# Two attention decode problems on one core: V loaded once per group, half of K and V from the Pool queue

## Chip, cores and metric

The kernel runs on one core of a Trainium2 chip. The metric is the device time in microseconds (us) of one execution, as the median of three runs; less is better.

## What is computed

The same computation is done on two independent sets of inputs, A and B, and the two results are put side by side.

```
B, Hq, Hkv, Sk, Dh, D = 2, 32, 16, 16384, 128, 576
W = 4096                                   # the last W positions of the caches
q = (x @ wq)                               # one query token per batch entry, 32 heads
k, v = k_cache[:, :, Sk-W:], v_cache[:, :, Sk-W:]   # each of 16 heads serves 2 query heads
scores = einsum("bhqd,bhkd->bhqk", q, k) * Dh**-0.5
o = einsum("bhqk,bhkd->bhqd", softmax(scores), v)
out = o.reshape(B, 1, Hq*Dh) @ wo          # bf16 throughout, x: [2, 1, 576], out: [2, 1, 576]
```

Nearly all bytes are K and V: 2 problems x 2 tensors x 2 batch entries x 16 heads x 4096 x 128 x 2 bytes, 134 MB of the 153 MB that are read.

## The kernel before

**Groups and slabs.** Four heads of one problem make a group; there are NG = 8 groups. A group has a K slab and a V slab for each of the two batch entries, so there are 16 K slabs and 16 V slabs of 4 MB. A slab fills 128 partitions with 32 KB each: partition (r, k) holds 128 consecutive positions of head k (line 370). Four slabs fit in the tile `ring` (NSLOT = 4). K and V take the four slots in turn.

**The stream.** All large loads are issued by SyncE (SP), in the order of the list `stream` (lines 322 to 332): the K slab of step t, then the V slab of step t-3 (LAG = 3), with the rows of `wo` ("M", 2.25 MB for two groups) in between, and at the end the `wo` rows of the last two groups ("W"). SP waits before each load for the last reader of the slot (line 373): the transpose of a K slab (`last_reader`, line 440) or the matmuls of a V slab (line 551). It issues strictly in this order, so one late reader holds up all loads behind it. Both `wq` (4.5 MB each) come first; they lie in the ring too, and the first K slabs wait for the query matmuls `f_q` that read them (`first_deps`, line 342).

**One K slab, step t** (loop at line 700). `make_X` (line 432): VectorE transposes each half of the slab in 32x32 blocks of fp32 pairs into `xt`. `make_S` (line 442): 16 TensorE matmuls for each half, with the queries in `zq` (which `make_Z` on GpSimd (POOL) writes), give the scores in PSUM, `STT`, one buffer for each of two groups.

**A group's softmax** starts when its second K slab is through. `make_max` (line 468): a maximum on VectorE, two small steps on POOL; `make_Tm_pe`, `make_nM`, `make_bias` (lines 475 to 495): two small TensorE transposes with a VectorE and a POOL step between them turn it into the bias of the exponential. Then ScalarE does four exponentials of 128x512 (line 500), which write `pR` and sums; `make_pT` (line 506) transposes `pR` on VectorE into `pT`, of which there are two; `make_sums` forms the divisors.

**A group's V.** `make_PV` (line 544) multiplies a V slab: 32 matmuls whose stationary part is 128x32, in four column groups of the array. `make_evac` (line 553) scales and sums the result on VectorE, `make_dg` and `make_pick` (lines 573, 582) sort it by head, and `make_projm` (line 622) multiplies by the `wo` rows. For the last two groups `make_proj` (line 645) does this at the very end, followed by the output in `make_E`.

**Order.** The program is written out by hand: each engine executes its own list in the order in which the helpers are called, and waits on semaphores. What stands behind a waiting instruction waits too, the loads on SP and the steps on POOL among them. The end of the program after the loop (lines 741 to 770) is also written out by hand. `filler` matmuls compute nothing that is used.

The DMA call for one slab:

```
return e.dma_start(ring[:, r, c0 * 128:c1 * 128],
                   src[:, :, c0:c1, :].rearrange("r k j d -> r k (j d)")).then_inc(sm, 16)
```

Of the kernel before, what the change touches and what calls it, by code (L numbers as in the profile page):

```python
# [5 lines left out]
FP32 = mybir.dt.float32  # L6
# [57 lines left out]
def build_kernel(nc, probs, out):  # L64
    NSLOT = 4
    LAG = 3
# [27 lines left out]
    with es:  # L94
# [5 lines left out]
        pR = sb("pR", [128, 2048], BF16)  # L100
        pT = sb("pT", [128, 2, 2048], BF16)
        tmp = sb("tmp", [128, 512], FP32)
        oR = sb("oR", [128, Bb, 128], FP32)
# [4 lines left out]
        ones_f = sb("ones_f", [128, 128], FP32)  # L108
        ones_b = sb("ones_b", [128, 128], BF16)
        sel = sb("sel", [128, 4, 128], BF16)  # L110
        bmask = sb("bmask", [128, 4], FP32)
        vmask = sb("vmask", [128, 4], FP32)
        offm = sb("offm", [128, 4], FP32)
# [4 lines left out]
        m8 = sb("m8", [128, 16, 8], FP32)  # L118
        selx = sb("selx", [128, 8, 16], FP32)
        selm = sb("selm", [128, 16, 8], FP32)  # L120
        bsel = sb("bsel", [128, 2], FP32)
        hmask = sb("hmask", [4, 2], FP32)
        mx = sb("mx", [128, 2], FP32)
        mv = sb("mv", [128, 2], FP32)
        m1 = sb("m1", [128, 1], FP32)
        nM = sb("nM", [1, 16], FP32)
        nMrep = sb("nMrep", [1, 8, 16], FP32)
        bias4 = sb("bias4", [128, 4], FP32)
        rsum4 = sb("rsum4", [128, 4], FP32)
        rsum8 = sb("rsum8", [128, 2, 4], FP32)  # L130
        ssum = sb("ssum", [128, 2], FP32)
        rsb = sb("rsb", [128, 2, 2], FP32)
        oP = sb("oP", [128, 2, 8, Bb], BF16)
        oM = sb("oM", [128, 16, Bb], BF16)
        out_sb = sb("out_sb", [Bb, NOUT], BF16)
        out_w = sb("out_w", [32 + Bb, NH], BF16)
# [12 lines left out]
        pTf = pT[:].rearrange("p v f -> p (v f)")  # L149
# [3 lines left out]
        assert XW + 512 <= 2 * 2048  # L153
# [5 lines left out]
        ring_sem = [sem("ring%d" % r) for r in range(NSLOT)]  # L159
        v_cuts = [0, 80, KJ]  # L160
        lastv_sem = [sem("lastv")]
# [61 lines left out]
        def turn_x(P):  # L223
# [5 lines left out]
            def f_xT(e, P=P):  # L229
                for k in range(4):  # L230
# [8 lines left out]
        d_dm = mask(dmask[:, 0:4], ident_f[:].rearrange("p (c j q) -> p j c q", j=4, q=8), AX.XY, "dmask")  # L239
# [4 lines left out]
        p_offm = pool(lambda e: e.tensor_scalar(offm[:], vmask[:], -1.0, OFF, ALU.add, ALU.mult), [d_vm], "offm")  # L244
        p_v2 = pool(lambda e: e.tensor_tensor(v2[:], vmask[:, 0:2], vmask[:, 2:4], ALU.add), [d_vm], "v2")
        p_m8 = pool(lambda e: e.tensor_copy(m8[:], jmask_f[:, 0:8].unsqueeze(1).broadcast_to([128, 16, 8])), [d_jf], "m8")
        p_sx = pool(lambda e: e.tensor_copy(selx[:], jmask_f[:, 0:8].unsqueeze(2).broadcast_to([128, 8, 16])), [d_jf], "selx")
        p_sm = pool(lambda e: e.tensor_copy(selm[:].rearrange("p (a h) c -> p a h c", a=2),
                                            jmask_f[:, 0:8].unsqueeze(1).unsqueeze(3).broadcast_to([128, 2, 8, 8])), [d_jf], "selm")
# [72 lines left out]
        stream = []  # L322
        for t in range(NSLAB + LAG):
            if t < NSLAB:
                stream.append(("K", t))
            if t >= LAG:
                i = t - LAG
                if i % 4 == 0 and i > 0:
                    stream.append(("M", i // 4 - 1))
                stream.append(("V", i))  # L330
        stream.append(("W", NG - 2))
        stream.append(("W", NG - 1))
        NM = NG // 2 - 1
        slot_of = {}
        uses = {}
        n_slot = 0
        for key in stream:
            if key[0] in "KV":
                slot_of[key] = (n_slot + 3) % NSLOT
                uses.setdefault(slot_of[key], []).append(key)  # L340
                n_slot += 1
        first_deps = {0: [q_done[0]], 1: [q_done[0], q_done[1]], 2: [q_done[1]], 3: []}
        stream_dma = {}
        last_reader = {}
# [4 lines left out]
        def issue(key):  # L349
# [18 lines left out]
            P, g, b = i // (2 * GP), (i // 2) % GP, i % 2  # L368
            src_t = probs[P][1] if kind == "K" else probs[P][2]
            src = src_t[b, 4 * g:4 * g + 4, Sk - W:Sk, :].rearrange("k (r j) d -> r k j d", j=KJ)  # L370
            r = slot_of[key]
            prior = uses[r][:uses[r].index(key)]
            deps = [last_reader[prior[-1]]] if prior else first_deps[r]
            cuts = [(0, KJ, ring_sem[r])]
            if key == ("V", NSLAB - 1):
                cuts = [(v_cuts[k], v_cuts[k + 1], ([ring_sem[r]] + lastv_sem)[k]) for k in range(2)]
            stream_dma[key] = []
            for c0, c1, sm in cuts:
                def f(e, c0=c0, c1=c1, sm=sm):
                    return e.dma_start(ring[:, r, c0 * 128:c1 * 128],  # L380
                                       src[:, :, c0:c1, :].rearrange("r k j d -> r k (j d)")).then_inc(sm, 16)
                stream_dma[key].append((c0, c1, dma_op("sp", sm, 1, f, deps, "%s%d_%d" % (kind, i, c0))))
# [6 lines left out]
        def filler(n):  # L389
            def f(e):  # L390
                o = STT[(NG - 1) % 2][:, 0:512]
                last = e.matmul(o, ones_b[:, :], xt[:, 0, 0:512], start=True, stop=True, skip_group_check=True)
                for _ in range(n - 1):
                    last = mm_held(e, o, ones_b[:, :], xt[:, 0, 0:512], True)
                return last
            pe(f, [exp_op[NG - 1], Xop[(NSLAB - 1, 1)]], "filler")
# [17 lines left out]
        def make_Z(t):  # L414
            P, g, b = t // (2 * GP), (t // 2) % GP, t % 2
            deps = [qs_ev, p_zq, d_bm]
            if t >= 2:
                deps.append(Sop[(t - 2, 1)])

            def f(e):  # L420
                for kp in range(2):
                    m = 2 * b + kp
                    b0 = zq[:, 0, m, 16 + 4 * m:16 + 4 * m + 1]
                    dst = bass.AP(b0.tensor, b0.offset, [list(b0.ap[0]), [4 * 144, 4], [32, 4], [1, 4]])
                    o = b * Hq + 8 * g + 4 * kp
                    src = qs[:, P, :].rearrange("d (p w) -> d p w", p=4)[:, :, o:o + 4].unsqueeze(2).broadcast_to([128, 4, 4, 4])
                    msk = bmask[:, 0:4].unsqueeze(1).unsqueeze(3).broadcast_to([128, 4, 4, 4])
                    last = e.tensor_tensor(dst, src, msk, ALU.mult)  # L428
                return last
            Zop[t] = pool(f, deps, "Z%d" % t)  # L430

        def make_X(t, jh):
            ensure(("K", t))
            r = slot_of[("K", t)]
            deps = [stream_dma[("K", t)][0][2], Sop[(t - 1, jh)] if t >= 1 else d_xT[1]]
# [6 lines left out]
        def make_S(t, jh):  # L442
# [3 lines left out]
            if b == 0 and G >= 2:  # L446
                deps.append(exp_op[G - 2])
# [32 lines left out]
        def make_nM(G):  # L480
            n, b = tm_job[G]
            op = ch[(G, "Tm")]
            nm = dve(lambda e: e.tensor_reduce(nM[0:1, 0:16], b[0:1, 0:128].rearrange("o (a w) -> o w a", a=8), AX.X, ALU.max, negate=True),
                     [op] + prev(G, "nMrep"), "nM%d" % G)
            tb_consumer[n] = nm
            ch[(G, "nMrep")] = pool(lambda e: e.tensor_scalar(nMrep[:], nM[0:1, 0:16].unsqueeze(1).broadcast_to([1, 8, 16]), SCALE, None, ALU.mult),
                                    [nm] + prev(G, "bias"), "nMrep%d" % G)

        def make_bias(G):
            n, bk, op = tb_job(lambda e, bank: e.transpose(bank[:, 0:1], nMrep[0:1].rearrange("o a w -> o (a w)"), ident_f[0:1, 0:1]),  # L490
                               "bias%d" % G, [ch[(G, "nMrep")], p_ident_f])
            ch[(G, "bias")] = op
            b4 = dve(lambda e: e.scalar_tensor_tensor(bias4[:], vmask[:], bk[:, 0:1], offm[:], ALU.mult, ALU.add),  # L493
                     [op, p_offm, d_vm] + ([exp_op[G - 1]] if G >= 1 else []), "bias4_%d" % G)
            tb_consumer[n] = b4
            st = STT[G % 2]

            def f(e):
                for kv in range(4):
                    last = e.activation(pR[:].rearrange("p (x k) -> p k x", k=4)[:, kv, :],  # L500
                                        st[:, :].rearrange("p (x t) -> p t x", t=2)[:, kv % 2, :], ACTF.Exp,
                                        bias=bias4[:, kv:kv + 1], scale=SCALE, accum_out=rsum4[:, kv:kv + 1])
                return last
            exp_op[G] = act(f, [b4] + prev(G, "rsum8") + ([pT_op[G - 1]] if G >= 1 else []), "exp%d" % G)

        def make_pT(G):
            v = G % 2
            deps = [exp_op[G]] + ([PVop[2 * (G - 2) + 1]] if G >= 2 else [qt_op])
            pT_op[G] = dve(lambda e: e.transpose(  # L509
                pT[:, v, :].rearrange("p (w j q) -> p j w q", w=4, q=8),  # L510
                pR[:].rearrange("p (j w q) -> p j w q", w=4, q=8)), deps, "pT%d" % G)

        def make_rsum(G):
            ch[(G, "rsum8")] = pool(lambda e: e.tensor_tensor(
# [38 lines left out]
        def make_evac(i):  # L553
# [6 lines left out]
            if i:  # L560
                deps.append(ch["tmp"])
# [301 lines left out]
```

## Time and profile before

| | |
|---|---|
| median of 3 runs | 363.31 us (363.24 to 363.34) |
| time of the profiled execution | 363.1 us |
| its span, first to last instruction | 361.8 us |
| mean granted TensorE clock | 0.887 of full speed |
| busy: PE, DVE, ACT, POOL | 229.0, 218.6, 45.4, 24.3 us |
| bytes read | 153.10 MB, 423 GB/s over the span |
| time that packets of SP's DMA queue took | 98.7% of 16 DMA engines' span |

The span is what the profile's clock runs over; the time of the execution is 1.3 us longer. Busy times are those in which an engine executes something; waits are not counted. A DMA is issued by an engine's queue and then carried out by 16 DMA engines in packets, one packet here being one contiguous row of a partition. "DMA share" is the mean share of time in which these 16 were busy. The profile's timeline lists each instruction with its start and duration, and in brackets how long the engine had been idle before it and for what. Durations below come from this one execution.

### The profile page before, as it was taken

The numbers are of one execution on the slowest core, as the hardware profiler recorded it, in microseconds if no ns is written. First come the engines' busy times: TensorE is split into PE (matmuls) and PEld (weight loads), VectorE is DVE, ScalarE is ACT, GpSimd is POOL, SyncE is SP. The second block draws the span as 40 slices with busy tenths as digits, with TensorE's granted clock in tenths as the row PEclk, the third lists the DMA queues.
The fourth block names the chain that finished last, engine by engine and source line by source line (L and its number), as shares of the span: only waits on it lengthen the run. The fifth ranks groups of instructions, "written<-read, shape, count | busy, mean of one in ns | idle before, by whom it ended". The sixth has DMA issues, their size and how long they took to land.

```text
span 361.8 us, 2701 instructions
## 1 busy us (share of the span) xinstructions
PE 229.0 (63%) x1357; PEld 56.1 (16%) x943; DVE 218.6 (60%) x150; ACT 45.4 (13%) x77; POOL 24.3 (7%) x84
## 2 busy tenths in 40 slices
PE   0397687767464866671696656662776675667575
PEld 0010111112110211120121211110112121112222
DVE  0811898495949392924919493952927776675522
ACT  1002100040031002200005000500005000500500
POOL 4200101100010001000010000000010000001000
PEclk9999698969999889888798998899589897869989
DMA  8999999999999999999999999999999999999996
GB/s 327 449 428 420 442 426 424 446 413 446 417 447 420 442 422 422 439 438 420 438 424 434 431 438 412 448 420 442 424 435 429 428 438 420 434 442 420 427 417 258
DMA packets 6088, 153.28 MB, mean 424 GB/s; under 512 B 684, under 2 KB 828, under 8 KB 1084
## 3 DMA queue, kind: packets, MB, share of 16 engines
q1 hardware_dynamic: 6056, 153.10, 98.7%
q8 instruction: 9, 0.15, 0.2%
q14 instruction: 3, 0.02, 0.0%
q10 hardware_dynamic: 20, 0.01, 0.0%
HBM read 153.10 MB, written 0.00 MB: 423 GB/s over the span
## 4 chain that ended last, share of the span: by engine, by line
DMA 49%; DVE 24%; PE 16%; issue 8%; ACT 1%; POOL 1%; SPq 0%
DMA ring<-in_B_k_cache_dram 25%; DVE xt L436 15%; DMA ring<-in_B_v_cache_dram 9%; DMA ring<-in_B_wq_dram 7%; DMA ring<-in_A_k_cache_dram 6%; PE st L266 6%; PE st L462 5%; DMA wob<-in_B_wo_dram 3%; DVE oR L569 2%; DVE mx L470 2%; DVE pT L509 2%; PE pj L266 2%; DVE tmp L562 2%; PE ot L539 1%; ACT pR L500 1%
## 5 line engine op out<-in xcount | busy, mean ns | idle before, releaser
L462 PE MATMUL st<-xt,zq 128*128 128x512 bf16 x256 | 119.3, 466 | 93.6 <-DVE xt L436 93.6
L436 DVE STREAM_TRANSPOSE xt<-ring 128x4096 f32<-128x4096 f32 x32 | 141.6, 4429 | 33.5 <-DMA ring<-in_A_k_cache_dram 18.2
L266 PE MATMUL st<-xt,zq 128*128 128x512 bf16 x256 | 118.0, 461 | 0.0
L500 ACT ACTIVATE pR<-st,bias 128x512 bf16<-128x512 f32 x32 | 40.0, 1419 | 219.0 <-DVE bias L493 219.0
L462 PEld LDWEIGHTS st<-xt,zq 128*128 128x128 bf16 x256 | 28.3, 110 | 211.5 <-DVE xt L436 110.0
L539 PE MATMUL ot<-ring,pT 128*32 128x512 bf16 x512 | 32.0, 393 | 8.3 <-DMA ring<-in_B_v_cache_dram 8.3
L493 DVE SCALAR_TENSOR_TENSOR bias<-vmask,tb,offm 128x4 f32<-128x4 f32 x8 | 1.8, 224 | 37.1 <-PE tb L490 37.1
L523 DVE TENSOR_REDUCE ssum<-tb 128x2 f32<-128x8 f32 x8 | 1.3, 162 | 33.4 <-PE tb L520 33.4
L428 POOL TENSOR_TENSOR zq<-qs,bmask 128x64 bf16<-128x64 bf16 x32 | 8.6, 292 | 161.2 <-PE st L266 140.3
L509 DVE STREAM_TRANSPOSE pT<-pR 128x2048 bf16<-128x2048 bf16 x8 | 18.4, 2303 | 0.7 <-ACT pR L500 0.7
L562 DVE SCALAR_TENSOR_TENSOR tmp<-ot,rsb,dmask 128x512 f32<-128x512 f32 x16 | 11.5, 719 | 9.4 <-PE ot L539 9.4
L281 PE MATMUL ot<-ring,pT 128*32 128x512 bf16 x18 | 7.6, 421 | 15.1 <-DMA ring<-in_A_wq_dram 14.5
L539 PEld LDWEIGHTS ot<-ring,pT 128*32 128x32 bf16 x512 | 12.4, 99 | 23.7 <-DMA ring<-in_B_v_cache_dram 10.5
L569 DVE TENSOR_REDUCE oR<-tmp 128x128 f32<-128x512 f32 x15 | 15.6, 1039 | 0.5
L266 PE MATMUL pj<-ring,pT 128*32 128x512 bf16 x36 | 12.1, 422 | 0.0
L266 PE MATMUL pj<-wob,oM 128*2 128x288 bf16 (+1 forms) x64 | 10.2, 256 | 0.0
L470 DVE TENSOR_REDUCE mx<-st 128x2 f32<-128x1024 f32 x8 | 9.7, 1208 | 0.1
L500 ACT ACTIVATION_READ_ACCUMULATOR pR<-st,bias 128x1 f32 x32 | 9.1, 283 | 0.0
L636 PE MATMUL pj<-wob,oM 128*2 128x288 bf16 x32 | 7.9, 286 | 0.0
L224 DVE TENSOR_TENSOR xt<-xt,hmask 4x1152 bf16<-4x1152 bf16 x2 | 2.8, 1398 | 8.4 <-DMA xt<-in_A_x_dram 8.4
L266 PE MATMUL st<-ring,pT 128*32 128x512 bf16 x18 | 7.4, 414 | 0.0
L472 POOL TENSOR_TENSOR mv<-mx,v 128x2 f32<-128x2 f32 x8 | 1.6, 195 | 80.0 <-DVE mx L470 80.0
(71 smaller groups left out, 79.5 us busy)
## 6 DMA issues: line engine op xcount, KB each, us to landing
ring<-in_A_k_cache_dram SPq DMA_DIRECT2D x8, 4096.0 KB, 24.9
ring<-in_A_v_cache_dram SPq DMA_DIRECT2D x8, 4096.0 KB, 30.0
ring<-in_B_k_cache_dram SPq DMA_DIRECT2D x8, 4096.0 KB, 28.5
ring<-in_B_v_cache_dram SPq DMA_DIRECT2D x7, 4096.0 KB, 31.8
ring<-in_A_wq_dram SPq DMA_DIRECT2D x1, 4608.0 KB, 13.6
ring<-in_B_wq_dram SPq DMA_DIRECT2D x1, 4608.0 KB, 24.1
wob<-in_A_wo_dram SPq DMA_DIRECT2D x2, 2304.0 KB, 29.8
ring<-in_B_v_cache_dram SPq DMA_DIRECT2D x1, 2560.0 KB, 26.9
```

Source lines behind the costliest of these rows:

```text
L266: return e.add_instruction(mybir.InstMatmult(name=nc.get_next_instruction_name(), engine=mybir.EngineType.PE, ins=[e.lower_ap(mv_), e.lowe ...
L281: last = e.matmul(QB[c], wt, mv_, start=first, stop=True, skip_group_check=True)
L428: last = e.tensor_tensor(dst, src, msk, ALU.mult)
L436: Xop[(t, jh)] = dve(lambda e: e.transpose(xt[:, jh, :].bitcast(FP32).rearrange("p (kp x kt) -> p x kp kt", kp=2, kt=2), ring[:, r, jh * H ...
L462: last = e.matmul(ob, wt, mv_, start=first, stop=True, skip_group_check=True)
L470: ch[(G, "max")] = dve(lambda e: e.tensor_reduce(mx[:], st[:, :].rearrange("p (x t) -> p t x", t=2), AX.X, ALU.max), [Sop[(2 * G + 1, 1)]] ...
L500: last = e.activation(pR[:].rearrange("p (x k) -> p k x", k=4)[:, kv, :], st[:, :].rearrange("p (x t) -> p t x", t=2)[:, kv % 2, :], ACTF.Exp,
L509: pT_op[G] = dve(lambda e: e.transpose(pT[:, v, :].rearrange("p (w j q) -> p j w q", w=4, q=8), pR[:].rearrange("p (j w q) -> p j w q", w= ...
L539: last = e.matmul(OTB[32 * c:32 * c + 32, :], pT[:, v, base + 32 * c:base + 32 * c + 32], ring[:, r, jj * 128:(jj + 4) * 128], start=rd == ...
L562: evac_op[i] = dve(lambda e: e.scalar_tensor_tensor(tv, o, rsb[:, v, b:b + 1], dm, ALU.mult, ALU.mult), deps, "ev%d" % i)
L569: ch[(G, "red%d" % b)] = dve(lambda e: e.tensor_reduce(oR[:, b, :], tmp[:].rearrange("p (j d) -> p d j", j=4), AX.X, ALU.add), [evac_op[i] ...
L636: last = e.matmul(PJ[0], oM[:, j, :], mv_, start=start and j == 0, stop=True, skip_group_check=True)
```

## The change

- **V per group.** A V load now covers both batch entries of a group: 64 partitions for each, 64 KB in each partition (256 positions), 8 MB in two slots of the ring. There is one place for V (slots 2 and 3), for the last group slots 0 and 1. K slabs are cut by halves of these 256 positions rather than by batch entry, and take two slots (0 and 1; the first slab slot 3).
- **Two queues.** Of each K and V load SP issues partitions 32 to 95 (batch entry 0). POOL issues partitions 0 to 31 and 96 to 127 (batch entry 1), as two DMAs (`edges`), in its own list of instructions and with the same waits. `wq`, `wo` and the output stay on SP (and ScalarE).
- **Order of the stream.** V of group G now stands behind K slab 2G+3, and `M` rows ahead of a K slab.
- **Order of work.** In the loop, a group's maximum, bias and exponentials, and the V matmuls of the group before, come right after its second K slab and ahead of the next K slab.
- **What follows from the mix of batch entries.** The exponentials are done once for each batch entry over all 128 partitions, with a mask in the bias (eight instead of four), and `pT` becomes one tile for both; its transposes double. V needs 64 matmuls a group as before, now with a stationary part of 128x64, in two column groups instead of four. Evacuation and its reduction are done once a group instead of twice. The pick has two reductions, `nM` and `nMrep` two steps each, `make_Z` four small steps instead of two; the POOL step `make_rsum` is gone.

The core of the diff:

```diff
-        for t in range(NSLAB + LAG):
...
+        stream = [("K", 0), ("K", 1), ("M", 0), ("K", 2)]
+        for G in range(NG - 2):
+            stream += [("K", 2 * G + 3), ("V", G)]
+            if G == 3:
+                stream.append(("M", 1))
+            stream.append(("K", 2 * G + 4))
+        stream += [("M", 2), ("K", NSLAB - 1), ("V", NG - 2), ("V", NG - 1), ("W", NG - 2), ("W", NG - 1)]
...
+                    return e.dma_start(place(key)[32:96, c0 * 128:c1 * 128], piece(key, 0, 0, 16, c0, c1)).then_inc(sm, 16)
+                stream_dma[key].append(dma_op("sp", sm, 1, f, data_deps(key), "%s%d_%d" % (kind, i, c0)))
...
+        def data_deps(key):
+            kind, i = key
+            if kind == "K":
+                return [[], [q_done[0]], q_done_all][i] if i < 3 else [last_reader[("K", i - 2)]]
+            if i == 0:
+                return q_done_all + [last_reader[("K", 0)]]
+            return [last_reader[("K", NSLAB - 2)], last_reader[("K", NSLAB - 1)]] if i == NG - 1 else [last_reader[("V", i - 1)]]
+
+        def edges(key):
...
+                for p0, r0 in ((0, 0), (96, 8)):
+                    def f(e, c0=c0, c1=c1, sm=sm, p0=p0, r0=r0):
+                        return e.dma_start(place(key)[p0:p0 + 32, c0 * 128:c1 * 128], piece(key, 1, r0, r0 + 8, c0, c1)).then_inc(sm, 16)
+                    op = dma_op("pool", sm, 1, f, data_deps(key) if key != ("K", 0) else [[wq_dma[0]], [q_done[0]]][p0 > 0], "%se%d_%d_%d" % (kind, i, c0, p0))
...
+        for k in range(NG - 1):
+            t = 2 * k + 1
+            make_K(t, 0)
+            make_K(t, 1)
+            if t + 2 < NSLAB:
+                edges(("K", t + 2))
+                make_Z(t + 2)
+            if k >= 1:
+                make_pT(k - 1, 0)
+                make_pT(k - 1, 1)
+                make_sums(k - 1)
+            make_max(k)
+            make_Tm_pe(k)
+            make_nM(k)
+            make_bias(k)
+            if k >= 1:
+                make_PV(k - 1)
+            edges(("V", k))
+            make_K(t + 1, 0)
+            if k >= 1:
+                make_evac(k - 1)
+                make_dg(k - 1)
+            make_K(t + 1, 1)
+            if k >= 1:
+                make_A(k - 1)
+            if t + 3 < NSLAB:
+                edges(("K", t + 3))
+                make_Z(t + 3)
+            if k >= 1:
+                make_pick(k - 1)
...
         T = NSLAB - 1
...
+        make_K(T, 0)
+        make_K(T, 1)
+        edges(("V", NG - 1))
+        make_pT(NG - 2, 0)
+        make_pT(NG - 2, 1)
+        make_sums(NG - 2)
+        make_max(NG - 1)
         make_Tm_pe(NG - 1)
         make_nM(NG - 1)
...
         make_bias(NG - 1)
...
+        make_PV(NG - 2)
+        make_pT(NG - 1, 0)
+        make_pT(NG - 1, 1)
+        make_evac(NG - 2)
         make_dg(NG - 2)
...
+        make_A(NG - 2)
         make_pick(NG - 2)
...
         make_sums(NG - 1)
...
         filler(4)
...
+        make_PV(NG - 1, (0,))
         filler(4)
...
+        make_PV(NG - 1, (1,))
         filler(3)
...
+        make_PV(NG - 1, (2,))
+        make_evac(NG - 1)
+        make_dg(NG - 1)
+        make_A(NG - 1)
+        make_pick(NG - 1)
         make_proj(NG - 2)
         make_proj(NG - 1)
```

`make_K` is `make_X` followed by `make_S`. The last V load is cut in three (144, 80 and 32 of 256 positions a partition); before, the last V slab was cut in two (80 and 48 of 128). With `make_X` of a slab the transposes now also wait for the POOL half of the load and for `make_Z` of that slab.

## The prediction

> **What bounds the kernel now.** I read the stretches first: does the load stream ever rest?
>
> ```profile
> core 0: us, PE busy (x) PEld busy (x) DVE busy (x) ACT busy (x) POOL busy (x), PEclk, DMA share, GB/s
> 2.00:315.00 313.00, 198.96 (x1044) 45.94 (x718) 195.07 (x119) 39.16 (x67) 21.74 (x71) 0.89 1.00 430
> 315.00:358.50 43.50, 28.72 (x281) 9.53 (x210) 23.05 (x30) 6.00 (x10) 1.31 (x5) 0.88 0.98 420
> ```
>
> The DMA engines are busy all of the time from 2 us to 315 us and nearly so to the end, at 430 GB/s. PE and DVE are not even two thirds busy. So the stream is the bound, and the readers matter only where they make it rest, or where they are late behind its last byte. For that end I read the chain of waits:
>
> ```profile
> 312.57 31.80 DMA ring<-in_B_v_cache_dram
> 344.41 3.19 PE ot L539 x30
> 348.13 0.33 SPq L364
> 348.51 10.90 DMA wob<-in_B_wo_dram
> 360.15 0.28 ACT out_w L688
> ```
>
> It ends on the last `wo` rows, landed at 359.4 us; 2.4 us later the span ends. The work behind V is just ahead of that load. Last, the DMA issues and the timeline, for where the last K slab stands:
>
> ```profile
> wob<-in_B_wo_dram SPq DMA_DIRECT2D x1, 2304.0 KB, 27.4
> ```
> ```profile
> 287.68 0.59 SPq L364 DMA_DIRECT2D wob<-in_B_wo_dram  x1
> ```
> ```profile
> 310.87 4.44 DVE L436 STREAM_TRANSPOSE xt<-ring 128x4096 f32<-128x4096 f32 x1
> ```
>
> The third `wo` load (M2), issued right behind the last K slab (K15), lands at 287.7 + 27.4 = 315.1 us. By then all of `wq`, K0 to K15, the first 12 V slabs and three M loads are in, 134 MB. K15 itself is in by 310.9 at the latest, since its transpose starts there. Behind 315.1 come 16.8 MB of V and 2.4 MB of `wo`.
>
> **The path that sets the end after the change.** M2 now stands ahead of K15 on SP. When K15 lands, the same 134 MB must have landed: 315.1 us at today's pace. From there I add up what must follow, in the order of the lists:
>
> - two transposes of K15, 8.8 (timeline: a pair takes 8.77);
> - 16 score matmuls behind the second, 3.9 at full clock (0.235 each); the two `pT` transposes of group 6 (2.3 each) lie beside them and end 0.7 later, then its sums and divisor, 0.8: 14.2;
> - maximum to exponential: 5.0 in the rows (329.31 to 334.31), less 1.5 for waits there behind V matmuls and an evacuation, plus a second `nMrep` step of 0.55: 18.3 (POOL first issues V7's six edges, 3 to 7.4 us from 8.8 on, when its step of the maximum is due at 15.5: 0 to 0.7 late);
> - eight exponentials instead of four, twice 4.95 (a set takes 4.99 in the chain): 28.2;
> - second `pT` transpose of group 7, 2.3: 30.5;
> - only then evacuation and reduction of group 6 (0.72 + 1.04), its `dg` and pick (1.9, from 338.4 to 340.3), sums and fillers (1.4) ahead of group 7's V matmuls on PE: 35.5;
> - 64 V matmuls and two fillers (1.75): see below, 9.3: 44.8;
> - evacuation to last pick, 2.9 in the rows (355.0 to 357.9), plus 0.35 for wider tiles: 48.0;
> - last `wo` products (1.2) and the end of the span (1.7): 51.
>
> About 14 us of it are PE's; at the mean granted clock of 0.89 they take 1.8 longer: I take 52, bounds 49 and 57 (half clock: score matmuls 0.43 each). The stream needs 19.1 MB / 430 = 44.5 behind K15, and 2.4 to the end, 47. So the compute chain, today beside the stream, is the later one by 5 us. Today K15 lands 5.5 us earlier, M2 coming behind it, half as many exponentials are in the chain, and group 6's V work is spread ahead of them.
>
> **V matmuls.** The form 128x64 is not in the trace. A set of 32 in four column groups takes 1.9:
>
> ```profile
> 310.68 1.87 PE ot L539 x32
> ```
>
> 64 cost 3.8 if pace stays, 15 if each runs alone (0.235). I take 7.6, two side by side, as the shape says: +3.8 a group. This lies beside the stream except in the tail, where it is counted.
>
> **The loop.** V has one place, so the next V load waits for the V matmuls of the one before. After V(G) lands the stream has two K slabs, 19.5 us, before it runs dry. The matmuls wait for the bias of the next group, 18.3 us after that group's second K slab, which landed 19.5 before V(G); a backlog of 2.5 on DVE puts them 1 to 2 us behind V(G)'s landing. With 7.6 and an issue of 0.5 to 1.3 the next V load starts after some 10 to 11: covered, 8 us to spare. Per group DVE gains 2.3 (`pT`), loses 1.8 (one evacuation and reduction less), and is at some 28 of 39 us; ACT gains 5 and stays under 11; POOL gains two DMA issues for each load (no such row; 0.5 as on SP, 1.24 as ACT's slowest) and 1.1 of small steps, all behind transposes that end earlier. I cost these at nothing; if the cover were gone, 3 to 4 us a group.
>
> **Stream, gain.** V rows of 64 KB halve V's packets, and a second queue might fill gaps between packets. Bounds: nothing, and 134 MB at 440 GB/s, the pace of the best 20 us (window 40 to 60): 304.5 + 2, 8.6 us earlier. The DMA share is 1.00 already, so I take 1.5. [...]
>
> **Stream, start.** POOL's first edges wait only for the first `wq` (landed 14.5), so they share DMA engines with the second `wq` and can delay it by 4.9 (2.1 MB at 430 GB/s), or by 0. Scores of slab 0 begin 39.6, slab 1's last transpose ends 54.1 (K4's issue on SP now); that becomes up to 59.0. SP issues K3 and, behind it, V0 only then; before, K3 went out at 33.4 and V0 at 43.9. What is issued by then, 24.4 MB, lasts until 2 + 56.7 = 58.7. With the issue I take 2 us of rest, bounds 0 and 4.5.
>
> **Stream, M loads.** Two queues with work take turns at a DMA engine, as the small loads of x on ACT's queue show beside 4.5 MB of `wq` on SP's:
>
> ```profile
> 1.92 1.24 ACTq L200 DMA_DIRECT2D xt<-in_A_x_dram  x1
> ...
> 9.91 1.34 DVE L224 TENSOR_TENSOR xt<-xt,hmask 4x1152 bf16<-4x1152 bf16 x1 [8.36 <-DMA xt<-in_A_x_dram]
> 14.49 0.10 PEld L281 LDWEIGHTS ot<-ring,pT 128*32 128x32 bf16 x1 [14.49 <-DMA ring<-in_A_wq_dram]
> ```
>
> x (4.5 KB) was issued after both `wq` (9.4 MB, 22 us of stream). It does not wait for them, but still takes 7 to 8 us, since each of its rows waits behind packets of 36 KB. M loads stand on SP alone. While SP's half of the queue works off M2, POOL's goes on with K15's edges and then V6's, so SP's half of K15 comes after much of V6's edges, up to 4.2 MB: 9.8 us later, with no byte saved. If the order of issue held, 0. The x rows point to the upper end, but POOL's half is issued later each time and may trail: I take 5. [...] M1 does the same to K10 and eats the 8 us to spare in the loop: 1, bounds 0 and 4.6.
>
> **Sum.** 315.1 + 2 (start) + 1 (M1) + 5 (M2) - 1.5 (gain) + 52 = 373.6 us of span. This execution took 363.1 for 361.8 of span, and the median is 363.31: +1.5. **375 us**, 3% slower.
>
> **Rivals.**
>
> 1. *K and V land in order of issue, only the tail is exposed.* No push by M2, none by M1: 315.1 + 1 - 1 + 52 + 1.5 = 369 (364 to 370). For it: SP issues earlier than POOL. Against it: the x rows.
> 2. *Faster: two queues stream better.* The place is the stretch from 2 to 315 us, the price 0.73 us for every GB/s over today's 428 (134 MB in 313.1 us). With the chain of 51 behind K15 the kernel is faster by 0.2% (under 362.6, span 361.1) once K15 lands by 310.1, 5 us earlier: from 435 GB/s, without a rest at the start or a push. At 440: 306.5 + 51 + 1.5 = 359. For it: 20-us windows at 439 and 440. Against it: a share of 1.00. [...]
> 3. *V matmuls one after another, or POOL's half starved.* PE then needs 15 a group, the next V load comes 18.5 after V(G)'s landing, M loads push it over 19.5, and the tail grows by 7.4: 386 to 395. The same if POOL's DMAs carry less than the change says, that is, if its half lands late because POOL issues it late. For it: PE is 63% busy and its clock falls. Against it: four column groups do run side by side now.
>
> **Chances.** Forecast (push by M2 of 2 to 10 us, 370 to 386) 0.50; rival 1, 0.28; rival 2 0.14, of which 0.04 within 0.2%; rival 3 0.08. The range 363 to 386 leaves out most of rivals 2 and 3. Faster by over 0.2% 0.10, within 0.2% 0.04, slower 0.86; 0.2% is about what a measurement of this kernel can tell from no change.
>
> **What would show it.** K15's first transpose starts at 317 to 328 us; the last V matmuls run after the last `wo` load has landed, and the chain of waits ends in ScalarE, DVE and PE, not in a DMA; the DMA share is 0 for the last 5 us or more. The start shows a stretch near 59 us with a share under 1. V matmuls of a group take 7 to 8 us. It is wrong if K15 lands before 312, if the exponentials of group 7 do not stand between K15 and the end, or if the DMA share in the loop falls under 0.95, which would mean that the loop, not the tail, costs the time.

## The result, and the profile after

The changed kernel takes 381.48 us (median of four executions), against 363.27 for the kernel before on the same chip: the ratio is 1.0485, 95% interval 1.044 to 1.053. One of the four (390.68 us; the others took 379.62 to 382.22), two of the four of the kernel e1 below, its profiled one (381.1 us) among them, and one each of e2 and e6 ran disturbed; they are left out of the ratios, but not of the medians. The forecast was 375, range 363 to 386. The profiled execution took 380.74 us, its span 379.5.

I read it in the order of the prediction. First the stretches of the kernel after, cut where the DMA share falls; the columns are busy time and instructions of the five engines, then granted clock, DMA share and GB/s.

```profile
2.00:315.00 313.00, 207.16 (x962) 59.17 (x654) 186.56 (x124) 66.13 (x113) 52.00 (x151) 0.85 0.97 414
...
56.00:66.00 10.00, 7.87 (x32) 1.54 (x16) 5.54 (x2) 0.00 (x0) 2.23 (x8) 1.00 0.68 270
66.00:108.00 42.00, 25.94 (x108) 7.39 (x78) 25.08 (x16) 15.89 (x27) 6.93 (x21) 0.76 1.01 436
108.00:118.00 10.00, 7.24 (x47) 2.73 (x35) 9.97 (x5) 3.63 (x8) 1.13 (x2) 1.00 0.84 337
118.00:188.00 70.00, 48.86 (x232) 15.31 (x170) 42.66 (x30) 16.53 (x27) 11.05 (x34) 0.85 1.00 431
188.00:198.00 10.00, 8.20 (x56) 3.27 (x44) 9.71 (x4) 2.94 (x6) 1.13 (x2) 1.00 0.80 323
...
274.00:284.00 10.00, 8.46 (x58) 3.43 (x46) 9.18 (x4) 5.04 (x10) 1.13 (x2) 1.00 0.85 336
...
370.00:379.50 9.50, 6.15 (x93) 2.88 (x55) 2.81 (x6) 0.28 (x1) 0.00 (x0) 1.00 0.04 13
```

The stream rests now: the share up to 315 us is 0.97 where it was 1.00, 9.4 us of 313. The table says where: 3.2 us near 61, 1.6 near 111, 2.0 near 192, 1.5 near 279. Between these places the pace is that of before, 431 to 436 GB/s. And in the last 9.5 us nothing is loaded any more (0.04). So there are two losses: about 9 us of rests on the way, and a tail in which only the engines work.

What lies at 111, 192 and 279? The timeline of after, matmuls of V and the loads issued behind them:

```profile
102.52 8.50 PE L574 MATMUL ot<-ring,pT 128*64 128x512 bf16 x64 [0.97 <-DMA ring<-in_A_v_cache_dram]
111.05 0.56 SPq L381 DMA_DIRECT2D ring<-in_A_v_cache_dram  x1
111.31 1.14 POOL L414 DMA_DIRECT2D ring<-in_A_v_cache_dram  x2 [10.04 <-PE ot L574]
...
182.65 9.39 PE L574 MATMUL ot<-ring,pT 128*64 128x512 bf16 x64 [1.76 <-DMA ring<-in_A_v_cache_dram]
192.06 0.56 SPq L381 DMA_DIRECT2D ring<-in_A_v_cache_dram  x1
```

These are the issues of V1 and V3 (V5 is the one at 278.33). Each waits for the V matmuls of the group before, since V has one place, and those waited for their own V slab to land. So V lands late. Which half of it? The increments of each load's semaphores, sixteen for a DMA, give the landing of both halves: V0's SP half landed at 82.4 us, its POOL half at 102.4; for V2 it is 171.9 and 182.5, for V4 250.1 and 269.7. **POOL's half trails SP's, by 0.2 to 20 us, through the whole kernel**, though POOL issues mostly 0.26 us after SP (V0, at 67.83 against 60.95 us, is an exception, so up to 7 of V0's 20 us are late issue). The page shows the same as medians from issue to landing (last column; KB are those of one DMA):

```profile
ring<-in_B_k_cache_dram SPq DMA_DIRECT2D x8, 2048.0 KB, 19.9
ring<-in_B_k_cache_dram POOLq DMA_DIRECT2D x16, 1024.0 KB, 27.8
```

The queues of the page tell why. Columns: packets, MB, share of the time of 16 DMA engines.

```profile
q1 hardware_dynamic: 3384, 85.99, 53.4%
q0 software_dynamic: 4160, 67.12, 41.4%
```

POOL's queue (q0) carries less than SP's (q1) in more packets. Of its 4,160 packets only 1,664 are data; 2,496 have four bytes. That is 48 for each of its 52 DMAs, on average three for each of the 16 DMA engines. SP's large DMAs have 16 each, one for each DMA engine. A four-byte packet takes 9 ns by itself; what it costs shows in two stretches of the DMA view, first 240 to 250 us, then 250 to 260:

```profile
DMA packets 174, 4.13 MB, mean 413 GB/s; under 512 B 90, under 2 KB 90, under 8 KB 90
...
q1 hardware_dynamic: 88, 3.74, 86.3%
q0 software_dynamic: 86, 0.39, 9.5%
```
```profile
q0 software_dynamic: 71, 3.21, 74.2%
q1 hardware_dynamic: 43, 1.11, 25.8%
```

V4's POOL half had been issued at 229.2 and both queues had work. Yet for 10 us POOL's queue moved 0.39 MB in 86 packets, 74 of them tiny, beside 88 packets of SP. The queues take turns here packet by packet, and a packet of four bytes uses up a whole turn, which lasts as long as SP's next packet, 2.42 us in the median for 64 KB. Only when the tiny ones are through does q0 move data (250 to 260 us: 3.21 MB). On average a K or V load costs POOL 10 turns on a DMA engine (4 packets of data, 6 tiny) and SP 5 (4 and 1).

The end, from the chain of waits of after:

```profile
321.92 0.60 POOL ring L414
322.52 28.25 DMA ring<-in_B_v_cache_dram
350.90 8.90 PE ot L574 x64
359.83 0.76 DVE tmp L589
...
369.16 2.28 PE ot L574 x20
...
372.19 1.00 PE ot L574 x8
...
377.89 0.28 ACT pR L717
```

The chain ends in PE, DVE and ACT, no longer in a DMA. Its last load is V6's POOL half, on which group 6's V matmuls wait until 350.90. K15 was in at 326.9 (POOL's half; SP's at 324.2) and its first transpose started at 328.86, when DVE was through with K14. V7 was in at 371.0, V7's last matmuls ran at 372.19, and the last `wo` row landed at 372.4. The span ends 7.1 us after that; before it was 2.0, for by its semaphore the last row of before landed at 359.8, and the 359.4 of the chain is the load ahead of it.

### The profile page after: what moved, and what is told of

It reads as the page before. It is cut to its first block, busy times and chain, and to the rows that moved or that the text cites. A ratio compares the mean times of both kernels' runs of the same rounds, so it can differ in the third digit from the quotient of the medians.

```text
span 379.5 us, 2874 instructions
## 1 busy us (share of the span) xinstructions
PE 255.5 (67%) x1359; PEld 78.5 (21%) x945; DVE 223.9 (59%) x156; ACT 83.4 (22%) x141; POOL 58.6 (15%) x171
## 3 DMA queue, kind: packets, MB, share of 16 engines
q0 software_dynamic: 4160, 67.12, 41.4%
## 4 chain that ended last, share of the span: by engine, by line
DMA 56%; DVE 23%; PE 17%; POOL 2%; issue 1%; ACT 0%; DVEq 0%; POOLq 0%
DMA ring<-in_B_k_cache_dram 24%; DMA ring<-in_A_k_cache_dram 22%; DVE xt L472 17%; DMA ring<-in_B_v_cache_dram 7%; PE ot L574 7%; PE st L284 4%; PE st L498 3%; DMA xt<-in_A_x_dram 2%; PE pj L284 2%; DVE oR L595 2%; DVE tmp L589 1%; POOL ring L414 1%; PE ot L299 1%; DVE pT L233 1%; DVE mrow L506 1%
## 5 line engine op out<-in xcount | busy, mean ns | idle before, releaser
L498 PE MATMUL st<-xt,zq 128*128 128x512 bf16 x256 | 112.0, 438 | 57.3 <-DVE xt L472 57.3
L542 ACT ACTIVATE pR<-st,bias 128x512 bf16<-128x512 f32 x64 | 77.9, 1430 | 223.9 <-DVE bias L535 223.9
L284 PE MATMUL st<-xt,zq 128*128 128x512 bf16 x256 | 110.9, 433 | 0.0
L574 PE MATMUL ot<-ring,pT 128*64 128x512 bf16 x448 | 63.8, 455 | 11.9 <-DMA ring<-in_A_v_cache_dram 6.7
L574 PEld LDWEIGHTS ot<-ring,pT 128*64 128x64 bf16 x448 | 32.7, 130 | 40.2 <-issue 27.0
L550 DVE STREAM_TRANSPOSE pT<-pR 128x2048 bf16<-128x2048 bf16 x14 | 31.2, 2269 | 0.0
L464 POOL TENSOR_TENSOR zq<-qs,bmask 128x32 bf16<-128x32 bf16 x64 | 13.2, 233 | 67.5 <-PE st L284 54.2
L299 PE MATMUL ot<-ring,pT 128*32 128x512 bf16 x18 | 7.8, 432 | 17.2 <-DVE bmask L220 14.6
L542 ACT ACTIVATION_READ_ACCUMULATOR pR<-st,bias 128x1 f32 x64 | 19.3, 301 | 0.0
L414 POOL DMA_DIRECT2D ring<-in_A_k_cache_dram x16 | 9.0, 565 | 39.5 <-DVE xt L472 27.5
L506 DVE TENSOR_REDUCE mrow<-st 128x2 f32<-128x1024 f32 x8 | 9.7, 1207 | 4.0 <-PE st L284 4.0
L414 POOL DMA_DIRECT2D ring<-in_A_v_cache_dram x8 | 4.5, 566 | 34.0 <-PE ot L574 33.8
```

Source lines behind the costliest of these rows:

```text
L284: return e.add_instruction(mybir.InstMatmult(name=nc.get_next_instruction_name(), engine=mybir.EngineType.PE, ins=[e.lower_ap(mv_), e.lowe ...
L299: last = e.matmul(QB[c], wt, mv_, start=first, stop=True, skip_group_check=True)
L414: return e.dma_start(place(key)[p0:p0 + 32, c0 * 128:c1 * 128], piece(key, 1, r0, r0 + 8, c0, c1)).then_inc(sm, 16)
L498: last = e.matmul(ob, wt, mv_, start=first, stop=True, skip_group_check=True)
L506: ch[(G, "max")] = dve(lambda e: e.tensor_reduce(mx[:], st[:, :].rearrange("p (x t) -> p t x", t=2), AX.X, ALU.max), [Sop[(2 * G + 1, 1)]] ...
L542: last = e.activation(pR[:, b, :].rearrange("p (x k) -> p k x", k=4)[:, kv, :], st[:, :].rearrange("p (x t) -> p t x", t=2)[:, kv % 2, :], ...
```

## Experiments

My theory after this reading, "turns": POOL's half trails because of its tiny packets, the late half delays V, and with V's single place that gives the rests; it makes V7 late as well. The first rival, "one place": the rests come from V's single place alone, whatever queue is behind. The second, my prediction's own account of the tail: the chain behind K15 sets the end. Ratios are to the kernel before, measured on the same chip beside each run (363.0 to 363.3 us); the share and the rate are those of the stretch 2 to 300 us.

| kernel | median us | ratio, 95% interval | DMA share, GB/s |
|---|---|---|---|
| before | 363.1 | 1 | 1.00, 430 |
| after | 381.48 | 1.0485 (1.044 to 1.053) | 0.97, 414 |
| e1: SP in halves | 379.48 | 1.037 (1.030 to 1.045) | 0.99, 423 |
| e2: POOL in halves | 562.69 | 1.545 (1.536 to 1.553) | |
| e3: M2 behind V6 | 382.59 | 1.052 (1.050 to 1.055) | |
| e4: before with two queues | 374.73 | 1.031 (1.027 to 1.035) | 0.99, 421 |
| e5: POOL in halves, by turns | 401.48 | 1.105 (1.104 to 1.107) | 0.93, 393 |
| e6: e1 and e3 | 373.54 | 1.026 (1.022 to 1.030) | 1.00, 427 |
| e7: e4, SP in halves | 368.80 | 1.017 (1.015 to 1.019) | 1.00, 426 |
| e8: e6, fewer exponentials | 373.36 | 1.029 (1.024 to 1.034) | |

### e1: as many turns for both queues

```diff
-                    return e.dma_start(place(key)[32:96, c0 * 128:c1 * 128], piece(key, 0, 0, 16, c0, c1)).then_inc(sm, 16)
+                    cm = (c0 + c1) // 2
+                    for a, b in ((c0, cm), (cm, c1)):
+                        last = e.dma_start(place(key)[32:96, a * 128:b * 128], piece(key, 0, 0, 16, a, b)).then_inc(sm, 16)
+                    return last
```

> After, with each K and V load of SP cut into two DMAs of half the columns (half-size packets, twice as many). Theory 'turns' (POOL's half trails because each of its DMAs brings three 4-byte packets to each DMA engine, and each of them waits a turn behind one of SP's big packets: 10 turns of POOL a load against 5 of SP): now both queues have 10 turns a load, the POOL half trails by under 3 us in place of 1 to 20, the rests before V1, V3 and V5 (6.5 us) go, and V7 lands earlier: 371 to 377 us. Rival 'one place' (the rests come from V's single place in the ring alone, whatever queue is behind): the rests stay at 6 to 7 us, 381 to 383 us.

The rests nearly went: 1.00 less 0.99 of the stretch to 300 us, where after has 0.97; near 192 there is none, near 111 none, near 272 1.6 us. POOL's and SP's median time to landing became equal (22.5 and 22.6 us; after: 26.6 and 21.0, over all loads). The last load landed at 365 us, after's at 372.4. V's single place is as it was, so "one place" falls: without the late half it costs almost nothing. POOL's DMAs are those of after, so a slow issue on POOL is not the cause either. But the ratio fell only from 1.0485 to 1.037, 4 us; by the ratio e1 takes 376.5 us, at the weak end of what was expected, and its median of 379.48 lies above it. The chain of waits of e1 says why:

```profile
294.76 31.24 DMA ring<-in_B_k_cache_dram
326.03 4.46 DVE xt L475
...
344.76 9.74 ACT pR L545 x16
```

K15, issued at 294.76, landed only at 326.03. POOL's half of it was in at 316.3; it was SP's half that came 9.7 us later, with M2 standing ahead of it on SP alone. It is the push that the prediction bounded at 9.8: by the packets of the trace POOL's queue had moved 2.7 MB of V6 by 326.0, 6.3 us at 430 GB/s. In after this push does not show, because POOL trails by more: when K15 landed, V6 had been issued for only 5 us. What the loop gained, the tail lost in part, in this execution all of it; e6 below bears this out.

### e2 and e5: more turns for POOL

e2 cuts POOL's loads in halves of the columns instead of SP's; e5 does the same in another order.

```diff
+                        cm = (c0 + c1) // 2
+                        for a, b in ((c0, cm), (cm, c1)):
+                            last = e.dma_start(place(key)[p0:p0 + 32, a * 128:b * 128], piece(key, 1, r0, r0 + 8, a, b)).then_inc(sm, 16)
+                        return last
```

e5 in its place:

```diff
+                cm = (c0 + c1) // 2
+                for p0, r0, a, b in ((0, 0, c0, cm), (96, 8, c0, cm), (0, 0, cm, c1), (96, 8, cm, c1)):
```

> After, with each K and V load of POOL cut into two DMAs of half the columns, SP's left whole. Theory 'turns': POOL now has 20 packets a load and engine (8 of data, 12 of 4 bytes) against 5 of SP; its half trails by 10 to 30 us, more rests in the stream, 388 to 402 us. Rival 'one place': two more issues of 0.55 us a load on POOL, the trail as it was, 381 to 384 us.

562.7 us: neither theory had this. The turns are there (POOL's median to landing rose to 37.7 us, SP's is 23.4), but something larger came on top. The DMA view of e2 from 485 to 500 us, where POOL's queue works alone:

```profile
DMA packets 226, 3.29 MB, mean 220 GB/s; under 512 B 121, under 2 KB 121, under 8 KB 121
...
q0 software_dynamic: 223, 3.29, 101.6%
```

All 16 DMA engines are busy (101.6%), and yet only 220 GB/s come, half the usual rate: the packets themselves are slow, 1182 ns in the median for 16 KB that take 611 in e1. The only thing new about them is that two DMAs to the same 32 partitions follow each other.

> As e2_pool_halves (562.7 us, where POOL's packets took twice their time: 1182 ns for 16 KB in place of 611), but the four POOL DMAs of a load in another order: partitions 0 to 31 and 96 to 127 by turns, not twice the one and then twice the other. Theory 'same partitions': in e2 two successive DMAs, each on half of the DMA engines, wrote to the same 32 partitions at one time and halved each other's pace; now the packets are back at 611 and 1213 ns. What is left is then the price of turns alone (20 POOL packets a load and engine against 5 of SP): 388 to 402 us. Rival 'one place': 381 to 384 us. If the packets stay slow the cause is not the order: 540 us or more.

With the two sets of partitions by turns the packets are back at their pace: from 250 to 270 us of e5 q0's 2.85 MB take 33.8% of the 16 engines, 2.4 us of all of them for a MB, where the 3.29 MB of the view of e2 take 4.6. The time is 401.5 us, at the upper end of what turns alone should give: 20 turns a load for POOL against 5 for SP raise the DMA share's loss to 7% of the stretch (0.93), in places of the same kind as in after: near the start and ahead of V loads (58 to 68, 116 to 122, 160 to 165, 290 to 294 us). So e2 was two effects, and e5 parts them. That the 32 partitions are the limit is inferred from this pair of runs.

### e4 and e7: the queue alone, in the kernel before

e4 is the kernel before with nothing changed but the queue of a part of each slab, so that the readers of a slab wait for both parts; e7 cuts SP's part in halves as e1 does.

```diff
-                    return e.dma_start(ring[:, r, c0 * 128:c1 * 128],
-                                       src[:, :, c0:c1, :].rearrange("r k j d -> r k (j d)")).then_inc(sm, 16)
+                    return e.dma_start(ring[32:96, r, c0 * 128:c1 * 128],
+                                       src[8:24, :, c0:c1, :].rearrange("r k j d -> r k (j d)")).then_inc(sm, 16)
...
+                for p0, r0 in ((0, 0), (96, 24)):
+                    def f(e, c0=c0, c1=c1, sm=sm, p0=p0, r0=r0):
+                        return e.dma_start(ring[p0:p0 + 32, r, c0 * 128:c1 * 128],
+                                           src[r0:r0 + 8, :, c0:c1, :].rearrange("r k j d -> r k (j d)")).then_inc(sm, 16)
+                    op = dma_op("pool", sm, 1, f, deps if key != ("K", 0) else [[wq_dma[0]], [q_done[0]]][p0 > 0], "%se%d_%d_%d" % (kind, i, c0, p0))
```

> Before, with nothing changed but the queue: of each K and V slab (32 KB rows, four places in turn) SP issues partitions 32 to 95 and POOL partitions 0 to 31 and 96 to 127 as two DMAs, each as soon as its place is free. Theory 'turns': POOL's half trails here as well, by 5 to 15 us (its 4-byte packets wait behind SP's 32 KB ones); the four places hide part of it, but the last V slab lands late behind the last wo rows: 365 to 373 us. Rival 'one place': two queues by themselves cost nothing that can be measured, 362 to 364.5 us, or gain up to 4 us if they fill gaps.

374.7 us, above the range of "turns" by 2: the second queue by itself costs 3.1%, about 11 us here, where the whole change costs 18. POOL issues mostly 0.26 us behind SP here too, but its median to landing is 23.1 us, SP's 14.4. Even four places in turn do not hide it all; the stretch 92 to 96 us, for example, of e4:

```profile
92.00:96.00 4.00, 2.95 (x13) 0.67 (x7) 0.99 (x1) 0.00 (x0) 1.15 (x2) 1.00 0.43 148
```

The last V slab, POOL's half, landed at 362.9, and the `wo` rows behind its readers at 369.4 (before: 359.8).

> As e4_before_two_queues (374.7 us), with each K and V load of SP cut into two DMAs of half the columns. Theory 'turns': the POOL half trails by under 3 us, the rests at 92 to 96 and 198 to 220 us go (3.6 us), and the last V slab lands earlier: 365 to 370 us. Rival 'a second queue costs by itself, however its turns stand': 373 to 376 us.

368.8 us: the turns account for about 5 of e4's 11 us (1.031 less 1.017 of 363). The share is 1.00 again. The rate is 426 GB/s, not 430: with a share of 1.00 this 1%, some 3 us, is no rest; the four-byte packets (3,168 on POOL's queue) may be part of it, which was not shown. The profiled execution (367.5 us, the fastest of the four) is 4.4 us longer than that of before, and at 358 us it is 1.3 MB behind, 3.1 us of stream. Where the rest of the 6 us that are left lies was not tried apart. After the M loads, which SP alone carries, it is now SP's half that trails (median to landing 24.1 us, POOL's 17.6).

### e3, e6 and e8: what sets the end

```diff
-        stream += [("M", 2), ("K", NSLAB - 1), ("V", NG - 2), ("V", NG - 1), ("W", NG - 2), ("W", NG - 1)]
+        stream += [("K", NSLAB - 1), ("V", NG - 2), ("M", 2), ("V", NG - 1), ("W", NG - 2), ("W", NG - 1)]
...
         make_PV(NG - 2)
+        make_projm(NG // 2 - 2)
```

> After, with the third wo load (M2) behind V6 in place of ahead of K15; the product with M2 runs behind the V matmuls of group 6. Theory 'chain behind K15' (as predicted: the compute chain behind K15 sets the end): K15 and V6 land 5.5 us earlier, and the end comes 4 to 5 us earlier, 376 to 378 us. Rival 'V7's late half' (the POOL half of V7 landed at 371.0 us and the last V matmuls began at 372.1, so the chain is only 1 us later than the stream): 379 to 381 us, unless V7's POOL half lands earlier as well.

K15 landed at 321.4 us instead of 326.9, the 5.5 us that M2's bytes take, and the time did not fall at all: 382.6 us, above both ranges (the ratio, 1.052, is in the interval of after). Rows of DVE, first of after, then of e3:

```profile
317.07 4.45 DVE L472 STREAM_TRANSPOSE xt<-ring 128x4096 f32<-128x4096 f32 x1 [4.62 <-DMA ring<-in_B_k_cache_dram]
...
328.86 8.77 DVE L472 STREAM_TRANSPOSE xt<-ring 128x4096 f32<-128x4096 f32 x2
...
356.54 2.31 DVE L550 STREAM_TRANSPOSE xt<-pR 128x2048 bf16<-128x2048 bf16 x1 [2.46 <-ACT pR L542]
```
```profile
316.66 4.45 DVE L472 STREAM_TRANSPOSE xt<-ring 128x4096 f32<-128x4096 f32 x1 [6.65 <-DMA ring<-in_B_k_cache_dram]
...
328.19 8.77 DVE L472 STREAM_TRANSPOSE xt<-ring 128x4096 f32<-128x4096 f32 x2
```

And the V7 rows of e3's chain:

```profile
355.81 2.31 DVE xt L550
...
363.22 4.77 PE ot L574 x32
...
372.00 1.00 PE ot L574 x8
```

K15's transposes (the rows x2) began only 0.7 us earlier, 6.8 us behind its landing. DVE had waited for K14 until 316.66: K14's POOL half landed at 316.6, SP's at 306.6. And the evacuation of group 5 stands between K14's two transposes. From the start of K15's transposes to the end it is 51.1 us (after: 50.6). So a chain through K15's transposes and the exponentials does set the end of e3, but it starts at K14's late half and not at K15's landing, and M2's place does not move that. V7 is close beside it: its POOL half lands at 370.8 as in after (371.0), 1.2 us ahead of its last matmuls. In after a third bound lies as close: V6's POOL half holds group 6's V matmuls until 359.8, and the chain behind K15 is through with its last `pT` at 358.85. So neither theory holds as it was written: in after the late POOL halves of V6 and V7 and a chain that starts at K14's meet within 1 to 2 us. K14's part is read from the traces, not tried by a run of its own.

e6 has both edits, e1's and e3's.

> After with both edits of e1 and e3: SP's loads in column halves and M2 behind V6. Theory 'M2 pushes SP's half of K15' (in e1 POOL's half of K15 landed at 316.3 us, SP's at 326.0, 9.7 us later, M2 standing between on SP): K15 is in by 316 to 319 us, the chain of 50 to 52 us behind it ends at 367 to 371, and V7, which M2 now pushes, lands by 365 with 8.5 us behind it, 373: 370 to 375 us. Rival 'the end is bound by something else than these two': 377 to 381 us, as e1.

373.5 us, in the range: e1 alone gave 4 us and e3 none, together they give 8. The trace is of its fastest execution (370.8 us). K14's halves landed at 302.0 and 302.2, K15's at 311.7 and 312.2, V7 at 359.5, and the share to 300 us is 1.00. The chain of e6:

```profile
311.79 4.35 DVE xt L475
317.16 8.77 DVE xt L475 x2
...
334.96 9.77 ACT pR L545 x16
...
352.86 5.25 PE ot L577 x33
```

K15's transposes start 11 us earlier than in e3, 5 us behind its landing, since DVE is still at K14 and the evacuation of group 5. V7's first cut (landed at 352.3) and the chain through the exponentials (V7's first matmuls at 352.86) meet within 1 us.

> As e6, but three of the four exponentials of the second batch entry of group 7 are left out (3.7 us of ScalarE's work in the chain behind K15). Theory 'chain': 3 to 4 us less than e6. Rival 'V7 sets the end': the same as e6 within 0.7 us.

No difference of 3 to 4 us (373.4 against 373.5, and the intervals overlap): with V7's matmuls starting when V7 lands (its first cut at 357.6, the matmuls at 357.69 in e8's trace, which is of its slowest execution, 376.1 us), a shorter chain of exponentials is worth nothing. None of these kernels beats the one before. What stays open: V's 64 KB rows and the new order of work without POOL's queue were not tried.

## Why the prediction came out as it did

The direction, the range and three of the signs named for it held (a chain that ends in engines, a share near 0 at the end, a rest near 59 us). Two signs did not: K15's first transpose started at 328.86 us, named 317 to 328, and the V matmuls of a group took 8.5 to 10.0 us, named 7 to 8. The sum was 6 us short, and three of its steps were wrong, in part against each other; that the miss is no larger is in part luck.

- **Start, 2 us (0 to 4.5).** Measured 3.2 in the stretch 56 to 66. Right.
- **Loop, "covered, 8 us to spare", with 1 for M1.** Measured 6 (9.4 of rests less the start). This is the step that failed most. It counted the reserve of 19.5 us from V(G)'s landing, as if all of it landed together and in order of issue. V0's late half landed at 102.4, SP's part of K5 at 106.9, so there was not half of it left. The matmuls took 8.5 to 10.0 us, predicted 7.6, but this alone was not the fault: in e1 they take as long (8.8 to 10.0 in the loop), and its rests behind the start are 1.6 us.
- **M2, push of K15, 5 us (0 to 9.8).** The mechanism is right: in e1 SP's half comes 9.7 us behind POOL's, with 6.3 us of V6 moved ahead of it. In after it is hidden, because POOL's half came later still: K15 landed at 326.9, which is 315.1 and the 9.4 us of rests and some 2 us of slower stream, and no push. The step named the wrong half as the late one.
- **Gain of 1.5 by a fuller stream.** None shows: with a share of 1.00 e6, which still has 64 KB rows in POOL's half, moves 427 GB/s and e7 426, the kernel before 430; over 313 us this is a loss of 2 to 3 us. A second issuing engine added no bandwidth in any of these runs (393 to 427 GB/s in the table).
- **Chain behind K15, 52 us (49 to 57).** 50.6 from the start of the transposes, and 2 for DVE, late with K14: right. But it was not the only bound. The prediction put the stream's side at 47, counting 2.4 us behind its last byte. In after V7 lands 44.1 behind K15, and its last matmuls, their evacuation and the products take another 8.5: 52.6, as long as the chain. V6's POOL half binds as well, by way of group 6's V matmuls (the chain of after). And where K15 comes earlier (e3), the chain starts from K14 instead.

K15 was predicted for 321.6 (315.1 and 2, 1, 5, less 1.5) and came 5.3 later, where the whole is 6 later. The loop's term was 5 too small and the stream's some 4 (2.4 lost, not 1.5 gained), the start's 1; M2's 5, which did not come due, cancel half of that. The sign that the prediction set for a loop that costs time, a share under 0.95, was set too low: 0.97 of 313 us is 9 us already.

Rival 3 had a late POOL half, "because POOL issues it late", at 386 to 395. POOL issued it mostly 0.26 us after SP, V0's alone 6.9 after; the half was late for another reason, and the cost was smaller. The row that could have told it was in the prediction: x, 4.5 KB, took 7 to 8 us because each of its rows waited a turn behind a packet of 36 KB, 1.36 us in the median. I read this for M's packets and not for POOL's small ones, which no row of before shows. In after there are on average three four-byte packets for each POOL DMA and DMA engine, and it is these that make POOL's 10 turns.

## What to carry to other kernels

In these runs two busy DMA queues shared the DMA engines by packets and not by bytes (240 to 250 us of after: 88 packets and 3.74 MB on SP's queue, 86 and 0.39 MB on POOL's). So count the packets of each load on each queue, the four-byte ones included: with 10 turns against 5 POOL's queue fell behind (median to landing 26.6 us against 21.0, after), with 10 against 10 it did not (22.5 against 22.6, e1). A load split over two queues was as late as its later half (V0 of after: 82.4 and 102.4 us, its matmuls from 102.52), so a reserve in a ring is to be counted from that one. What stood on one queue alone pushed only that half: M2 put SP's half of K15 9.7 us behind POOL's in e1; with M2 behind V6 (e6) the halves landed 0.5 apart. Before a long chain is shortened or started earlier, look whether another landing meets it at the same time, or keeps the engine that has to start it: e3 alone and e8 gave nothing, e1 and e3 together 8 us.

## What the hardware showed unexpectedly

- Each of POOL's DMAs in after has 48 packets of four bytes (2,496 for 52), on average three for each DMA engine; a large one from SP has 16. Beside SP's 64 KB packets each cost a turn of up to 2.4 us.
- Two successive POOL DMAs to the same 32 partitions ran at half the pace: 1182 ns for 16 KB in place of 611, 220 GB/s with all DMA engines busy (e2). By turns with another 32 partitions they ran at full pace: 2.4 us of all DMA engines for a MB in place of 4.6 (e5).
- The kernels with two queues differed more from one execution to the next: e7 took 367.5 to 369.9 us, the kernel before beside it 363.0 to 363.1.
